# An attention and maxout kernel whose order of work is set by a table per pair of groups

## The chip, the cores and the metric

The kernel runs on one core of one Trainium2 chip. The metric is the device time of one execution in microseconds (us); the median of three runs before the change is 2021.88 us (2021.07 to 2022.24). The core has TensorE (PE, matrix products into PSUM), VectorE (DVE), ScalarE (ACT), GpSimd (POOL, which reaches SBUF only) and SyncE (SP, whose queue issues all DMAs here). Each engine works through its own instructions in program order and waits on semaphores for the others.

## The reference

Pooled attention, and its output goes through a maxout layer:

```python
kv_pool = kv.reshape(B, H // 4, 4, W // 4, 4, C).mean(axis=(2, 4))   # 4 batches, 768 keys of 128
k = v = kv_pool.reshape(B, -1, C) @ w_sr
s = (q @ k.transpose(0, 2, 1)) / sqrt(C)                             # 12288 queries per batch
a = exp(s - s.max(-1)); a /= a.sum(-1) + 1e-09
x = (a @ v).reshape(49152, 128)
h = max(max(x @ w1, x @ w2), x @ w3)                                 # 768 hidden units
out = h @ w_out
```

## The kernel before

**Precision.** PE works on float16 pairs: each float32 operand is split into a high and a low half, and three products (high-high, high-low, low-high) stand for one. The maxout is rewritten with differences against w1, so that two products, a relu and a max give the hidden values, and a product w1 w_out (`w1o`) is added in the projection.

**Tiling.** The queries form 96 groups of 512 (24 per batch); a group has 4 tiles of 128 queries and its hidden layer 6 steps of 128 units. Each piece of work is a short token, and `step` (L851) and `start` (L948) turn a token into instructions:

- S: scores of a tile, 6 matmuls of 384 columns into one of two score buffers (`ps_s`). m: maximum and bias on DVE (`mx`, `nb`). e: exponential on ACT (`a<-ps_s`), which frees the score buffer. c: high half (`ahl<-a`) on ACT, or on DVE where the token has an exclamation mark. l: low half (`ahl<-a,ahl`) on POOL, or on DVE with the mark, and then SP issues the DMA transpose of the tile (`aT<-ahl`).
- X: half of a group's product with the values, 9 matmuls of 512 columns into `ps_x`; it needs the transposes of all four tiles. xh and xl: its high half on ACT and low half on DVE.
- H: a hidden step, 6 matmuls of 512 columns into the two buffers `ps_h`. R: relu of the first on ACT; M: max with the second on DVE; C: high half (`hh`) on ACT; L: low half (`hl`) on POOL, or on DVE with the mark. O: projection of a step, 3 matmuls of 512 columns into `ps_o` (6 at a group's last step).
- P: the finished group is copied out of PSUM by DVE (`o_planes`) and SP issues a DMA transpose of it. G: the two planes are merged by DVE (`o_sb<-o_turned`). T: it is scaled by DVE (`rs`, then `o_sb<-o_sb,w_down,rs`) and stored.
- qd, qc, qp, qe, qh, ql: load of q for two groups, scaling of its columns (POOL), its size (DVE: the largest absolute value), the exponent's scale, and the high and low halves with a DMA transpose (`qT`). k: a part of the preparation of the next batch's keys, by place (`keys_step`, L999). Tokens of `START` that begin with w prepare the weights, and kv, add, fold, gat, end and gathered the first batch's keys.

All instructions of the engines are recorded through one helper, so that nearly all rows of the profile name L103. Matmuls and everything else keep the program's order on each engine (`InOrder`, L95), so the tables set the order.

**Order before.** `START` (L169) brings the first two groups into flight. Then a loop (L1041) goes through groups 2 to 95 and six steps of each; row `g % 2 * 6 + f` of `ORDER` (L155) holds the tokens of that step. Some tokens act on all that is waiting (c, l, C, L), S is left out in steps 1 and 4 and X acts only there, and k looks up what part of the key work belongs to this step: two kv tiles of 512 KB a group, in the first 6 groups of a batch, the sums in its groups 3 to 8.

**The end.** The last group's last hidden step is done in two halves (`last_hidden`, L694). Its projection (`last_project`, L722) has the hidden values as the stationary operand and `w` with both halves as 256 moving columns, so that the sums with w's high half and with its low half stand side by side in PSUM; `last_finish` (L805) copies one out on ACT, adds on DVE, scales and stores. Two projections stand between `last_hidden` and the one that needs its values.

Of the kernel before, what the change touches and what calls it, by code (L numbers as in the profile page):

```python
# [9 lines left out]
F32 = mybir.dt.float32  # L10
# [10 lines left out]
def kernel(  # L21
# [101 lines left out]
    def times(t, src, by, by2=None):  # L123
# [29 lines left out]
    W_SIGNS = 3  # L153
    HB_ = 5
    ORDER = (  # L155
# [12 lines left out]
    )  # L168
    START = (  # L169
# [328 lines left out]
    st = {x: {} for x in ("q", "qr", "ps", "qT", "sc", "sm", "nb", "aT", "x", "hp", "h", "a", "turned", "split", "qhl", "xh")}  # L498
# [13 lines left out]
    def q_peak(s, summed=False):  # L512

        assert s < 2 or next_q["cols"] >= 2 * s + 2
# [207 lines left out]
    def last_project(g, f):  # L722

        (fh, fn), n = divmod(f, NFT // 2), NJ // 2
        h = st["h"].pop((g, f))
        chunks = [(h, wo[fh][:, fn])]
        if f == 0:
            chunks.insert(0, (st["x"][g], w1o))
            st["o"] = [
                ps.rearrange("p (j s c) -> p j s c", s=2, c=C)  # L730
                for ps in (ps_o.tile([C, G], F32, name="ps_o"), ps_x.tile([C, G], F32, name="ps_x"))
            ]
        for part, o in enumerate(st["o"]):
            for m, (h, w) in enumerate(chunks):
                hh, hl = h[part] if isinstance(h, list) else h
                off = 0 if isinstance(h, list) else part * n
                for i, h_ in enumerate((hh, hl)):
                    for j in range(n):
                        mm(
                            out=o[:, j], lhsT=h_[:, (off + j) * P:(off + j + 1) * P], rhs=w,  # L740
                            start=(f == 0 and m == 0 and i == 0 and j == 0),
                            stop=(f == NFT - 1 and i == 1 and j == n - 1),
                        )
# [61 lines left out]
    def last_finish(g, rs):  # L805
        osb, n = op.tile([P, NJ, C], F32, name="o_sb"), NJ // 2
        for part, o in enumerate(st["o"]):
            half = slice(part * n, (part + 1) * n)
            lo = hp.tile([P, G], F32, name="h1", bufs=2)[:, :n * C].rearrange("p (j c) -> p j c", c=C)
            act.copy(out=lo, in_=o[:, :, 1])  # L810
            dve.tensor_tensor(out=osb[:, half], in0=o[:, :, 0], in1=lo, op=ALU.add)
            dve.scalar_tensor_tensor(
                out=osb[:, half], in0=osb[:, half], scalar=w_down,
                in1=rs[:, half].unsqueeze(2).to_broadcast([P, n, C]), op0=ALU.mult, op1=ALU.mult,
            )
            store(g, part * n, osb[:, part * n:(part + 1) * n])
# [17 lines left out]
    to_max, to_exp, to_hi, to_lo, to_merge, to_scale = [], [], [], [], [], []  # L834
    to_relu, to_h, to_hh, to_hl, to_xh, to_xl = [], [], [], [], list(range(NG)), []
    to_hidden, to_project = ([(g, f) for g in range(NG) for f in range(NFT)] for _ in range(2))
    next_q = {"load": 0, "cols": 0, "peak": 0, "exps": 0, "hi": 0, "lo": 0}
    nxt = None

    def turn(what, last):  # L840
        n = next_q[what]
        if n >= last:
            return None
        next_q[what] += 1
        return n

    def some(queue, one):
        for _ in range(1 if one else len(queue)):
            yield queue.pop(0)

    def step(token, g, f, one=False, on=None):  # L851

        if token == "H":
            gf = to_hidden.pop(0)
            hidden(*gf)
            to_relu.append(gf)
        elif token == "R":
            for gf in some(to_relu, one):
                to_h.append((gf, hidden_first()))
        elif token == "M":  # L860
            for gf, h1 in some(to_h, one):
                st["h"][gf] = hidden_max(h1)
                to_hh.append(gf)
        elif token == "C":
            for gf in some(to_hh, one):
                hidden_hi(*gf)
                to_hl.append(gf)
        elif token == "L":
            for gf in some(to_hl, one):
                hidden_lo(*gf, on)  # L870
        elif token == "O":
            project(*to_project.pop(0))
        elif token == "S":
            if (one or f not in (1, 4)) and tiles:
                to_max.append(tiles.pop(0))
                scores(*to_max[-1])
        elif token == "X":
            if (one or f in (1, 4)) and products:
                g, part = products.pop(0)
                (attend if g else attend_tile)(g, part)  # L880
        elif token == "m":
            for t in some(to_max, one):
                soft_max(*t)
                to_exp.append(t)
        elif token == "e":
            for t in some(to_exp, one):
                soft_exp(*t)
                to_hi.append(t)
        elif token == "c":
            for t in some(to_hi, one):  # L890
                soft_hi(*t, on)
                to_lo.append(t)
        elif token == "l":
            for t in some(to_lo, one):
                soft_lo(*t, on)
        elif token == "xh":
            if to_xh:
                attended_hi(to_xh[0])
                to_xl.append(to_xh.pop(0))
        elif token == "xl":  # L900
            for x in some(to_xl, one):
                attended_lo(x)
        elif token == "P":
            if g > 0:
                turn_out(g - 1)
                to_merge.append((g - 1, g * NFT + f))
        elif token in ("G", "T"):
            if token == "G":
                n = g * NFT + f
                while to_merge and (one or to_merge[0][1] < n - 1 or g == NG - 1 and f == NFT - 2):  # L910
                    m = to_merge.pop(0)[0]
                    merge(m)
                    to_scale.append(m)
            else:
                for m in some(to_scale, one):
                    scale_out(m, finish_scale(m))
        elif token == "qd":
            s = turn("load", NG // 2)
            if s is not None:
                q_load(s)  # L920
        elif token == "qc":
            q = turn("cols", NG)
            if q is not None:
                q_cols(q, on)
# [167 lines left out]
```

## Time and profile before

| | |
|---|---|
| median of three runs | 2021.88 us |
| profiled execution, its own time | 2023.5 us |
| its span, first to last instruction | 2021.7 us |
| mean granted TensorE clock | 0.998 |
| busy PE / DVE / ACT / POOL | 98% / 74% / 72% / 70% |
| DMA moved | 283.30 MB, mean 140 GB/s |

The busy share of PE counts each matmul with a modelled end, so it is nearer to 100% than its real occupation. A row of a group of instructions reads: line, engine, operation, output and inputs by the program's names, shapes and count; then the time in which at least one of them ran, the mean of one in ns, and the engine's idle time just before them with what ended it. A row of the timeline starts with its time from the span's start and its length.

### The profile page before, as it was taken

The numbers are of one execution on the slowest core, as the hardware profiler recorded it, in microseconds if no ns is written. First come the engines' busy times: TensorE is split into PE (matmuls) and PEld (weight loads), VectorE is DVE, ScalarE is ACT, GpSimd is POOL, SyncE is SP. The second block draws the span as 40 slices with busy tenths as digits, with TensorE's granted clock in tenths as the row PEclk, the third lists the DMA queues.
The fourth block names the chain that finished last, engine by engine and source line by source line (L and its number), as shares of the span: only waits on it lengthen the run. The fifth ranks groups of instructions, "written<-read, shape, count | busy, mean of one in ns | idle before, by whom it ended". The sixth has DMA issues, their size and how long they took to land.

```text
span 2021.7 us, 29151 instructions
## 1 busy us (share of the span) xinstructions
PE 1971.2 (98%) x9797; PEld 963.3 (48%) x9797; DVE 1503.6 (74%) x2469; ACT 1454.0 (72%) x2530; POOL 1406.7 (70%) x1059
## 2 busy tenths in 40 slices
PE   5899999999999999999999999999999999999998
PEld 4444444444444444444444444444444444444444
DVE  7878877767777886777776888677777777777675
ACT  3767777777777677777777777777777777777774
POOL 2667767777767677777777677767776777777764
PEclk9999999999999999999999999999999999999999
DMA  7697766666677867666767876676666766676662
GB/s 252 124 189 169 140 129 131 137 131 125 139 161 165 171 130 136 129 128 131 141 123 165 169 175 130 120 136 134 138 124 127 136 136 125 126 138 133 130 119 65
DMA packets 839959, 283.30 MB, mean 140 GB/s; under 512 B 813440, under 2 KB 814592, under 8 KB 839808
## 3 DMA queue, kind: packets, MB, share of 16 engines
q1 hardware_dynamic: 839808, 281.43, 68.7%
q8 instruction: 77, 1.26, 0.2%
q14 instruction: 74, 0.61, 0.1%
HBM read 53.54 MB, written 25.17 MB: 39 GB/s over the span
## 4 chain that ended last, share of the span: by engine, by line
PE 80%; DVE 7%; DMA 5%; ACT 4%; issue 2%; POOL 2%; SPq 0%; DVEq 0%; ACTq 0%; POOLq 0%
PE ps_h L103 31%; PE ps_o L103 17%; PE ps_x L103 17%; PE ps_s L103 15%; DMA aT<-ahl 4%; DVE h L103 1%; POOL ahl L103 1%; DVE q_row L103 1%; ACT ahl L103 1%; ACT a L103 1%; DVE mx L103 1%; ACT xh L103 1%; ACT hh L103 1%; ACT h L103 1%; DVE rs L103 1%
## 5 line engine op out<-in xcount | busy, mean ns | idle before, releaser
L103 POOL TENSOR_TENSOR ahl<-a,ahl 128x768 f16<-128x768 f32 x383 | 628.3, 1651 | 305.6 <-issue 170.9
L103 POOL TENSOR_TENSOR hl<-h,hh 128x512 f16<-128x512 f32 x572 | 666.5, 1176 | 179.8 <-ACT hh L103 179.2
L103 DVE SCALAR_TENSOR_TENSOR h<-ps_h,h 128x512 f32<-128x512 f32 x575 | 396.5, 690 | 185.2 <-ACT h L103 94.7
L103 ACT ACTIVATE h<-ps_h 128x512 f32<-128x512 f32 x575 | 341.8, 594 | 247.2 <-PE ps_h L103 243.9
L103 ACT CAST hh<-h 128x512 f16<-128x512 f32 x577 | 349.6, 615 | 165.1 <-DVE h L103 165.0
L103 DVE TENSOR_REDUCE mx<-ps_s 128x1 f32<-128x768 f32 x384 | 366.1, 953 | 112.1 <-PE ps_s L103 111.2
L103 PE MATMUL ps_h<-xh,d_hi 128*128 128x512 f16 x1150 | 436.9, 380 | 2.5 <-DVE w1o L103 2.5
L103 PE MATMUL ps_h<-xh,d_lo 128*128 128x512 f16 x1150 | 436.7, 380 | 0.0
L103 PE MATMUL ps_h<-xl,d_hi 128*128 128x512 f16 x1150 | 436.4, 379 | 0.0
L103 ACT ACTIVATE a<-ps_s,nb,q_sc 128x768 f32<-128x768 f32 x384 | 378.4, 988 | 57.2 <-DVE nb L103 51.9
L103 PE MATMUL ps_x<-aT,v_hi 128*128 128x512 f16 (+1 forms) x1188 | 375.0, 373 | 15.6 <-DMA aT<-ahl 13.8
L103 PE MATMUL ps_s<-k_hi,qT 128*128 128x384 f16 x1536 | 375.3, 326 | 5.7 <-ACT a L103 4.9
L103 PEld LDWEIGHTS <-d_hi 128*128 128x128 f16 x2308 | 226.3, 98 | 257.3 <-issue 2.5
L103 PE MATMUL ps_o<-hh,wo 128*128 128x512 f16 x1140 | 339.0, 379 | 0.0
L103 PEld LDWEIGHTS <-qT 128*128 128x128 f16 x2304 | 225.6, 98 | 196.2 <-issue 8.3
L103 ACT CAST ahl<-a 128x768 f16<-128x768 f32 x379 | 310.3, 832 | 4.8 <-DMA aT<-ahl 0.4
L103 PEld LDWEIGHTS <-wo 128*128 128x128 f16 x1710 | 167.3, 98 | 191.7 <-issue 0.4
L103 PE MATMUL ps_s<-k_lo,qT 128*128 128x384 f16 x768 | 250.8, 327 | 0.3 <-DVE k_lo L103 0.3
L103 PE MATMUL ps_x<-aT,v_lo 128*128 128x512 f16 (+1 forms) x594 | 220.4, 373 | 0.0
L103 PE MATMUL ps_o<-hl,wo 128*128 128x512 f16 x570 | 216.0, 379 | 0.1
L103 POOL TENSOR_TENSOR q_sb<-q_sb,col_row 128x512 f32<-128x512 f32 x94 | 124.3, 1323 | 103.3 <-DMA q_sb<-in_q_dram 103.3
L103 PEld LDWEIGHTS <-v_hi 128*128 128x128 f16 x1188 | 115.4, 98 | 149.6 <-issue 9.6
(136 smaller groups left out, 1413.5 us busy)
## 6 DMA issues: line engine op xcount, KB each, us to landing
q_sb<-in_q_dram SPq DMA_DIRECT2D x48, 512.0 KB, 4.4
kv_piece<-in_kv_dram SPq DMA_DIRECT2D x48, 512.0 KB, 4.8
out_dram<-o_sb SPq DMA_DIRECT2D x95, 256.0 KB, 2.2
aT<-ahl SPq DMA_TRANSPOSE x384, 4.0
kv_piece<-in_moe_w_dram SPq DMA_DIRECT2D x6, 384.0 KB, 6.9
qT<-q_hl SPq DMA_TRANSPOSE x96, 3.4
o_turned<-o_planes SPq DMA_TRANSPOSE x95, 3.3
kv_piece<-in_moe_w_out_dram SPq DMA_DIRECT2D x2, 384.0 KB, 9.3
```

The source lines that it names most:

```text
L103: return lambda **kw: tc.keep_in_program_order(op(**kw))
```

## The change

The loop over groups and `ORDER` go. `START` has another order of the same kinds of work, up to group 4's second score. `STEADY` holds the tokens of one pair of groups and is run 45 times (NG // 2 - 3); `END` holds the rest. Each token now does exactly one piece of work.

The key work is told by two tokens: kd loads one kv tile (groups 1 to 12 of a batch; two kd stand side by side in each pair), and ka does one of three parts a group, by `KEYS_AT`. The sums lie in groups 3 to 15, the rest up to group 19.

The size of q in `STEADY` and `START` is qp!: the sum of absolute values, by an ACT instruction (Abs with accumulation) that the kernel had and did not use. In `STEADY` two of a pair's eight c are on DVE (c!) and two of its twelve L (L!).

In `last_project` the high and low halves of `w` go into the same PSUM region in turn: three products of 128 columns for the two of 256. `last_finish` scales straight from PSUM. Five projections now follow `last_hidden` ahead of the one that needs it.

```diff
-    ORDER = (
-        "H e C l L m k R c M X O S qc",
-        "H C R O G c L m M S l e qc k X",
-        "H l P L C T c R O m M e S X k",
-        "H C L R m M l X S e O c k",
-        "H L S C m l R M O c e X k",
-        "H m C xh l xl R c e M L S O qp k X",
-        "H C m l R M e k c L X O S",
-        "H C G R l L O m M c S k X e",
-        "H l P L k C R T e M m O S X c",
-        "H L C qh R m M l X O S e k ql c",
-        "H L m qh R l M c e X S O k C ql",
-        "H xh m C L xl l c e R M O S X k qd",
-    )
-    START = (
-        "wd.2.1 wm.2.1 sr qd qc! ws.2.1 wl.2.1 qc wd.0.0 qp qd wd.0.1 qh wm.0.1!",
...
+    KEYS_AT = ((3, 5, 6, 7), (8, 9, 10, 11), (12, 13, 14, 15))
+    START = (
+        "sr qd wd.1.1 wm.1.1 qc! ws.1.1 wd.0.1 wm.0.1 wl.1.1 ws.0.1 wd.2.1 wn.1.1 wl.0.1 qc",
+        "qp! wd.2.0 wm.2.1 ws.2.1 wd.3.0 wn.0.1 wr.1.1! wm.3.0 wl.2.1 ws.3.0 wn.2.1 qh wd.1.0 wm.1.0",
+        "ws.1.0 wm.2.0! wr.2.1 wd.0.0 wm.0.0! wl.1.0 ws.2.0 ws.0.0 wl.3.0 wl.0.0 wl.2.0 wn.1.0 kv.0.0 kv.2.0",
+        "kv.2.1 turn_w1.1 wn.0.0 wr.1.0 wt.0.0 wn.2.0 add.2.0.1 wt.1.0 gat.0.0.4 kv.0.1 gat.0.1.4 wr.2.0 kv.2.2 qd",
+        "kv.2.3 qh turn_w1.0 kv.0.3 fold.2.0.2 gat.2.0.2 wt.2.0 dsize.0 wt.2.1 fold.2.2.2! gat.2.2.2 wt.1.1 wt.0.1 dsize.1",
+        "dsized.0 wh.2.0 kv.1.0 kv.0.2 kv.1.1 dsized.1 wh.2.1 wh.1.0 fold.2.3.2.1! gat.2.3.4.0 kv.1.2 kv.1.3 gat.1.0.4 add.0.2.3",
+        "end.0.2.4 wn.3.0 end.2.3.2.1 wd.3.1 ql add.1.1.2 gathered.2 gathered.0 wm.3.1 wo.2.0 ql gathered_peak.0 kd qc",
+        "gat.1.1.4 wo.1.0 ws.3.1 gathered_peak.2 wl.3.1 end.1.3.4 gathered_peak.1 turn_tops qc qp! gathered.1 gathered_project.1 tops sized",
+        "qe qd qh qc gathered_project.0 gathered_hi.0 gathered_project.2 gathered_hi.1 gathered_lo.0 qh gathered_lo.1 S ql S",
...
+    )
+    STEADY = (
+        "H kd kd qc m S ka R c O M L! l H",
+        "G e qp! c S R m M qh l X e C X",
+        "H L O L O O C R c! L m xh xl S",
+        "e c M C H m S R M H e l l C",
+        "m R c e c L O O S ka ka M H L",
+        "P l l m C O R M H ka R M L e",
+        "X H R ql T G C O X T C qh M L!",
+        "L C c! S xh xl H R M O H R m qe",
+        "S l M O C L C ka m L qd ql L H",
+        "R O M e O P c H R l ka e C M",
+        "qc S C",
+    )
+    END = (
...
+        "C H P R M C L L L L L T last_hidden O",
+        "O O G T last_project.3 last_project.4 last_project.5 last_finish",
     )
...
-                ps.rearrange("p (j s c) -> p j s c", s=2, c=C)
-                for ps in (ps_o.tile([C, G], F32, name="ps_o"), ps_x.tile([C, G], F32, name="ps_x"))
+                ps[:, :n * C].rearrange("p (j c) -> p j c", c=C)
+                for ps in (ps_o.tile([P, G], F32, name="ps_o"), ps_x.tile([P, G], F32, name="ps_x"))
...
-                for i, h_ in enumerate((hh, hl)):
+                for i, (h_, s) in enumerate(((hh, 1), (hh, 0), (hl, 0))):
                     for j in range(n):
                         mm(
-                            out=o[:, j], lhsT=h_[:, (off + j) * P:(off + j + 1) * P], rhs=w,
+                            out=o[:, j], lhsT=h_[:, (off + j) * P:(off + j + 1) * P], rhs=w[:, s],
...
-            lo = hp.tile([P, G], F32, name="h1", bufs=2)[:, :n * C].rearrange("p (j c) -> p j c", c=C)
-            act.copy(out=lo, in_=o[:, :, 1])
-            dve.tensor_tensor(out=osb[:, half], in0=o[:, :, 0], in1=lo, op=ALU.add)
             dve.scalar_tensor_tensor(
-                out=osb[:, half], in0=osb[:, half], scalar=w_down,
+                out=osb[:, half], in0=o, scalar=w_down,
...
+    def keys_load(b, r):
+        if r == 1:
+            KT[b] = Keys(b)
+        if r <= KS * R:
+            KT[b].load(*divmod(r - 1, R))
...
+    def keys_step(b, r, n):
+        k = KT.get(b)
+        sums = {
+            KEYS_AT[s][i]: (s, what) for s in range(KS) for i, what in enumerate(((0, 1), (2, 3), (0, 2), "pool"))
+        }
+        if n < KU and r in sums:
+            s, what = sums[r]
+            if what == "pool":
+                k.pool(s, n)
+            else:
+                k.add(s, *what, us=slice(n, n + 1))
+        after = {
+            (KEYS_AT[0][3], 2): lambda: k.peak(0), (KEYS_AT[1][3], 2): lambda: k.peak(1),
+            (12, 2): lambda: k.turn(0), (13, 0): lambda: k.turned(0),
+            (KEYS_AT[2][3], 2): lambda: (k.peak(2), k.turn(1)), (16, 0): lambda: k.turned(1),
+            (16, 2): k and k.turn_tops, (17, 0): k and k.tops, (17, 1): k and k.sized,
+            (17, 2): lambda: k.project(0), (18, 0): lambda: k.projected(0),
+            (18, 2): lambda: k.project(1), (19, 0): lambda: (k.projected(1), k.value(0), k.value(1)),
+        }
...
     KT[0] = Keys(0)
+    run(START)
+    for _ in range(NG // 2 - 3):
+        run(STEADY)
+    run(END)
```

More of the change, by code (lines that the diff above doesn't have):

```diff
@@ L833 @@
     products = [(0, j) for j in range(NJ)] + [(g, part) for g in range(1, NG) for part in range(2)]
[L834 to L856, printed above, removed]
+    steps = [(g, f) for g in range(NG) for f in range(NFT)]
+    halves_q, eights_q = (list(range(n)) for n in (NG, NG // 2))
+    next_keys = [(b, r) for b in range(1, B) for r in range(1, GPB + 1)]
+    todo = {
+        "S": list(tiles), "X": products, "H": steps[:-1], "O": steps[:-3], "P": list(range(NG - 1)),
+        "xh": list(range(NG)), "qd": list(eights_q), "qc": list(halves_q), "qp": list(eights_q),
+        "qe": list(eights_q), "qh": list(halves_q), "ql": list(halves_q), "kd": list(next_keys),
+        "ka": [(b, r, n) for b, r in next_keys for n in range(3)],
+        **{t: [] for t in ("m", "e", "c", "l", "R", "M", "C", "L", "xl", "G", "T")},
+    }
@@ new lines, with step @@
+    FOLLOWS = {"S": "m", "m": "e", "e": "c", "c": "l", "H": "R", "R": "M", "M": "C", "C": "L", "xh": "xl", "P": "G", "G": "T"}
+    def step(token, on=None):
+        if not todo[token]:
+            return
+        n = todo[token].pop(0)
+        if token == "S":
+            scores(*n)
+        elif token == "m":
+            soft_max(*n)
+        elif token == "e":
+            soft_exp(*n)
+        elif token == "c":
+            soft_hi(*n, on)
+        elif token == "l":
+            soft_lo(*n, on)
+        elif token == "X":
+            (attend if n[0] else attend_tile)(*n)
+        elif token == "xh":
+            attended_hi(n)
+        elif token == "xl":
+            attended_lo(n)
+        elif token == "H":
+            hidden(*n)
@@ L857, in step @@
         elif token == "R":
[L858 to L859 removed]
+            st["h1"][n] = hidden_first()
         elif token == "M":
[L861 to L863 removed]
+            st["h"][n] = hidden_max(st["h1"].pop(n))
         elif token == "C":
[L865 to L867 removed]
+            hidden_hi(*n)
@@ L868, in step @@
         elif token == "L":
-            for gf in some(to_hl, one):
-                hidden_lo(*gf, on)
+            hidden_lo(*n, on)
         elif token == "O":
[L872 to L902, printed above, removed]
-        elif token == "P":
[L904 to L916, printed above, removed]
@@ L917, in step @@
+            project(*n)
+        elif token == "P":
+            turn_out(n)
+        elif token == "G":
+            merge(n)
+        elif token == "T":
+            scale_out(n, finish_scale(n))
         elif token == "qd":
-            s = turn("load", NG // 2)
-            if s is not None:
-                q_load(s)
+            q_load(n)
         elif token == "qc":
-            q = turn("cols", NG)
-            if q is not None:
-                q_cols(q, on)
+            q_cols(n, on)
@@ L948, in start @@
     def start(token):
-        nonlocal nxt
         k, on = KT[0], dve if token[-1] == "!" else None
@@ L981, in start @@
             AIDS[name](*n)
-        elif name == "nk":
-            r, f = n
-            if nxt is None:
-                nxt = Keys(1)
-            keys_step(r, f)
         else:
-            step(name, *(n or (1, 0)), one=True, on=on)
+            step(name, on)
     WEIGHTS = {
@@ L1036 @@
-    KT[0] = Keys(0)
-    for row in START:
-        for token in row.split():
-            start(token)
-    for g in range(2, NG):
-        r, b = g % GPB, g // GPB + 1
-        if r == 1 and b < B:
-            nxt = Keys(b)
-        for f in range(NFT):
-            if g == NG - 1 and f == NFT - 1:
-                break
-            for token in ORDER[g % 2 * NFT + f].split():
-                step(token, g, f)
-            if g == NG - 1 and f == NFT - 2:
-                step("G", g, f)
-                step("T", g, f)
-                rs = finish_scale(NG - 1)
-            if nxt and r == 17 and f == 4:
-                KT[b], nxt = nxt, None
@@ L1065, with run @@
+    def run(rows):
+        for row in rows:
+            for token in row.split():
+                start(token)
+    KT[0] = Keys(0)
+    run(START)
+    for _ in range(NG // 2 - 3):
+        run(STEADY)
+    run(END)
+    assert not any(v for t, v in todo.items() if t[0] != "k")
 _INS = ["q", "kv", "w_sr", "moe_w1", "moe_w2", "moe_w3", "moe_w_out"]
```

84 lines of the change are left out of this document (20 added, 64 removed), and 50 rows, old and new, of tables (END, START, STEADY).

## The prediction

> **What bounds the kernel now.** I read the engine totals first, then TensorE's (PE's) busy time in stretches that follow the stages.
>
> ```profile
> PE 1971.2 (98%) x9797; PEld 963.3 (48%) x9797; DVE 1503.6 (74%) x2469; ACT 1454.0 (72%) x2530; POOL 1406.7 (70%) x1059
> ```
> ```profile
> 0.00:39.20 39.20, 21.74 (x139) 20.26 (x140) 30.22 (x64) 8.59 (x17) 8.87 (x12) 1.00 0.82 289
> 39.20:59.00 19.80, 13.53 (x127) 9.45 (x127) 17.08 (x40) 14.32 (x26) 13.06 (x8) 1.00 0.79 143
> 59.00:100.00 41.00, 37.78 (x185) 18.57 (x183) 33.56 (x57) 28.60 (x53) 22.10 (x16) 0.96 0.60 112
> 100.00:590.00 490.00, 485.54 (x2389) 233.88 (x2388) 370.14 (x604) 360.16 (x625) 350.44 (x264) 1.00 0.72 143
> 590.00:700.00 110.00, 105.53 (x510) 50.05 (x509) 86.40 (x134) 76.96 (x135) 78.06 (x58) 0.98 0.82 172
> 700.00:1990.00 1290.00, 1281.51 (x6305) 616.99 (x6304) 949.39 (x1544) 952.01 (x1653) 923.32 (x696) 1.00 0.68 135
> 1990.00:2021.70 31.70, 25.57 (x149) 14.13 (x147) 16.85 (x29) 13.32 (x25) 10.82 (x9) 0.96 0.15 45
> ```
>
> Columns: stretch, length, then busy us of PE, weight loads, VectorE (DVE), ScalarE (ACT), GpSimd (POOL), PE's granted clock, DMA share, GB/s. PE sets the end. Its work hardly changes, so the change can win only PE's idle time: 17.5 us before the first score (39.2), 6.3 to the first hidden step (59), 3.2 to 100, 17.4 in the long middle (4.46 + 4.47 + 8.49), 6.1 at the end: 50.5 in all, plus lost clock (0.96 of 41 us is 1.6 us, 0.98 of 110 is 2.2).
>
> Who ends PE's waits in the middle (first view) and in the first 100 us (second):
>
> ```profile
> PE ps_x L103 <- DMA aT<-ahl: 12.0, 13, 2.5
> PE ps_x L103 <- DVE pool_max L103: 3.4, 3, 1.1
> ```
> ```profile
> PE ps_s L103 <- DVE kv_piece L103: 12.3, 2, 11.0
> PE ps_h L103 <- DVE w1o L103: 2.5, 1, 2.5
> ```
>
> The middle's stalls are X (attend) waiting for the last transpose of the probabilities. The chain of waits shows an unstalled pair of groups, and the late transposes:
>
> ```profile
> 530.79 1.94 PE ps_x L103 x9
> ...
> 570.96 1.94 PE ps_x L103 x9
> 572.91 1.29 PE ps_h L103 x6
> 574.20 0.97 PE ps_s L103 x6
> ...
> 580.04 1.29 PE ps_o L103 x6
> ...
> 638.11 5.55 DMA aT<-ahl
> 679.36 7.16 DMA aT<-ahl
> ```
>
> From the same X of one pair to the next is 40.17 us, and that is all PE work: 12 H of 1.29, 8 S of 0.97, 4 X of 1.94, 10 O of 0.65 and 2 of 1.29. So the repeated table cannot beat 40.17 either. In the queue of SyncE the late transpose stands behind loads:
>
> ```profile
> 675.87 0.89 SPq L103 DMA_DIRECT2D kv_piece<-in_kv_dram  x1
> 676.87 1.25 SPq L103 DMA_TRANSPOSE qT<-q_hl  x1
> 678.17 0.57 SPq L103 DMA_DIRECT2D q_sb<-in_q_dram  x1
> 679.36 2.26 SPq L103 DMA_TRANSPOSE aT<-ahl  x1
> 681.67 1.71 SPq L103 DMA_DIRECT2D kv_piece<-in_kv_dram  x1
> ```
> ```profile
> aT<-ahl SPq DMA_TRANSPOSE x384, 4.0
> ```
>
> The median is 4.0; with a kv tile and q ahead it took 7.16, and the clock fell after it (0.98 in that stretch's row).
>
> **Middle: the repeated table.** Durations that I use:
>
> ```profile
> L103 POOL TENSOR_TENSOR ahl<-a,ahl 128x768 f16<-128x768 f32 x383 | 628.3, 1651 | 305.6 <-issue 170.9
> L103 DVE TENSOR_REDUCE mx<-ps_s 128x1 f32<-128x768 f32 x384 | 366.1, 953 | 112.1 <-PE ps_s L103 111.2
> L103 ACT ACTIVATE a<-ps_s,nb,q_sc 128x768 f32<-128x768 f32 x384 | 378.4, 988 | 57.2 <-DVE nb L103 51.9
> L103 ACT CAST ahl<-a 128x768 f16<-128x768 f32 x379 | 310.3, 832 | 4.8 <-DMA aT<-ahl 0.4
> L103 DVE COPY o_planes<-ps_o 128x1024 uint16<-128x1024 uint16 x95 | 115.9, 1220 | 24.1 <-PE ps_o L103 23.6
> ```
> ```profile
> 2008.81 0.38 PE L103 MATMUL ps_h<-xh,d_hi 128*128 128x512 f16 x1
> ```
> ```profile
> 2009.72 0.60 ACT L103 ACTIVATE h<-ps_h 128x512 f32<-128x512 f32 x1 [1.57 <-PE ps_h L103]
> ```
>
> Even groups: PE work between the group's last S and its first X was 4 H + 2 S + 1 X + O worth 3.9, or 13.0 us; in the new table it is 5 H + 3 S + 2 X + O worth 4.5, or 17.8. The chain m, e, c, l, transpose is 0.95 + 0.2 + 0.99 + 0.2 + 0.83 + 1.65 + 4.0 = 8.8 without queueing, so these waits should vanish.
>
> Odd groups are the tight ones. Their last exponential (row 10 of the table) stands on ACT behind the R of the H before it. From that H's start: R at 0.9 (rows 2008.81 and 2009.72), e at 1.5, c at 2.7, l ends near 5.2. But SyncE takes its issues in program order, and P (turn_out), now in the same row, comes first: its O ends at 3.2, the copy to planes (1.22) near 4.65, its issue about 1.25 (row 676.87), so the last aT is issued at 5.95 and lands at 9.95. X is due after 4 H, 3 S and O worth 2.6: at 10.7. That leaves 0.7 us: a landing of up to 4.7 us is free. No q load stands just ahead any more (it is issued a row earlier, right behind tile 2's transpose), and the two kv tiles of a pair ("kd kd") follow behind. So I expect most of these waits to go as well.
>
> The row 681.67 shows a kv load behind the transpose that took 7.16, which by itself would make kd dangerous; the loads ahead explain it as well. The Trainium skill, page "DMA: Bandwidth & Descriptors", section "Queues, rings and completion order", says that descriptors on one engine are consumed in ring order; by that rule loads behind cost nothing, and without it 18 pairs (36 tiles) would each pay up to 2.5 us.
>
> Two more places have little room. S of tile 3 needs the score buffer of tile 1: ACT does C, R, c and e ahead of it, free at about 3.5, due at 4.2. Each second H half needs M done; the tightest (H 3 of the odd group, behind P and m on DVE) has 0.2. A key sum ("ka") stands ahead of two M's in the same rows. The top reduction of the keys moves behind an S, so the three waits on pool_max (3.4) go.
>
> What the middle can give: 17.4 idle, about 3 that the modelled ends of the waits hide (0.38 a matmul for 0.216 of issue) and some 1.5 of lost clock: 22. Bounds: 0 (each wait stays) and -22. I take **-17**, leaving 5 for the tight places in groups with key work. "VectorE apart from GpSimd" I cost at nothing: it shortens DVE steps such as this one, which no PE wait names.
>
> ```profile
> 1034.93 2.27 POOL L103 TENSOR_TENSOR hl<-h,hh 128x512 f16<-128x512 f32 x2
> ```
> ```profile
> 1036.04 1.19 DVE L103 TENSOR_SCALAR rs<-sm,o_down 128x4 f32<-128x4 f32 x1
> ```
>
> DVE's step over four columns ends just as POOL's two do, at 1037.2. What hides it is PE's 40.17 of work; uncovered, one such 1.19 in each of 46 pairs would cost 55. GpSimd's waits for q, which the earlier issue takes away, are as far from the path: 0.
>
> **qp!** puts the row sums of |q| on ACT (Abs with accumulation over 1024) in place of DVE's 1.21 reduction. No row shows it. Below: DVE gains 1.2, PE nothing. Above: nearest is a<-ps_s, 0.99 + 0.2 for 768; I take 1.2 a pair. Behind it on ACT stand c and R; the next H is 4.9 us of S and X away, so 0. If ACT had to swap function tables, the row is
>
> ```profile
> L103 ACT ACT_TABLE_LOAD x1 | 1.3, 1283 | 0.7 <-PEq L1076 0.7
> ```
>
> twice a pair, 2.6 us, which delays R and the xh that the next group waits for by about 0.5 to 1: 23 to 46 in all. The Trainium skill, page "ScalarE: Activation LUTs", section "Table sets: the hidden batching unit", says that abs is in every set; by it there is no swap, and no run so far shows it.
>
> **Start.** Before the first S, DVE is 30.2 busy. The new table adds there four tops (2.2), sizes (1.6), two d_lo (2.0), one low part, two scales and so on (1.5), and takes away two q reductions (2.4), two folds (1.1), one q scaling (0.7), one top (0.5): net +2.5, 32.7 of the 36.5 that DVE has after its first load at 2.7. One weight load fewer stands ahead of the last kv tile: 0.38 MB at 289 GB/s, 1.4 us. First S near 37.3: -2. After it DVE sheds about 7 of its 17.1 to the first H, where PE idles 6.3: -2.5. The rest to 100 us, with the w1o wait of 2.5: -1.5. **-6**; bounds +7 (the added DVE work in full, and POOL's folds late) and -11.
>
> **End.** Last projection: 56 matmuls of 256 columns become 84 of 128.
>
> ```profile
> 2012.29 0.38 PE L103 MATMUL ps_o<-wo,hh 128*128 128x256 f16 x2
> 2012.51 0.38 PE L103 MATMUL ps_o<-wo,hl 128*128 128x256 f16 x2
> ...
> 2015.89 0.39 PE L103 MATMUL ps_o<-wo,hh 128*128 128x256 f16 x2 [1.37 <-ACT hh L103]
> ...
> 2016.80 0.38 PE L103 MATMUL ps_x<-wo,hl 128*128 128x256 f16 x2
> ```
> ```profile
> 2018.56 0.48 DVE L103 SCALAR_TENSOR_TENSOR o_sb<-o_sb,w_down,rs 128x256 f32<-128x256 f32 x1
> ```
>
> 56 at 0.109 is 6.1; half the columns at half that, 84 x 0.055, is 4.6: -1.5 (0 if weight loads bind). From PE's end (2017.2) to DVE's (2019.04) is 1.85; without copy and add about 0.6: -1.2. The wait of 1.37 came from DVE, which reached the last hidden step late; five projections now stand between that step and the projection that needs it, instead of two: -1.4. Group 94's merge and scaling now stand ahead of the finish on DVE, about 2 us beside those projections. With a third of the lost clock (0.96 of 31.7 is 1.3) I take **-4.5**; bounds -6 and 0.
>
> **Sum.** 2021.7 - 17 - 6 - 4.5 = 1994.2 of span. The profiled execution took 2023.5, 1.8 more than its span and 1.6 more than the median 2021.88, so **1994.4** on the median's scale.
>
> **Rivals.**
> - *B, the stalls stay*: the odd X still waits as often as now. For it: 0.7 us of room. Against: no load ahead. 2021.9 - 6 - 4.5 = 2011.4. Chance 0.13.
> - *C, a slower start*: DVE binds before the first S (+7) with the rest as forecast: 2021.9 + 7 - 17 - 4.5 = 2007.4. For it: 32.7 of 36.5. Chance 0.10.
> - *D, slower*: P's transpose ahead of the last aT makes its landing late in each pair. Each 0.1 above 4.7 costs 46 x 0.1 = 4.6. It decides from 5.3 (28 us); at 5.5 (as row 638.11) 37 us: 2031. For it: the order on SyncE. Against: median 4.0. Chance 0.10, and a further 0.05 for landings near 5.3, which just cancel the gain (2022).
> - *E, ACT swaps tables*: 1994.4 + 35 = 2029. Chance 0.02.
>
> **How the numbers follow.** The forecast has 0.60; its own range is 1987 to 2003. 0.2% is 4 us, about what can be told from no change. Faster: 0.60 + 0.13 + 0.10 = 0.83; same 0.05; slower 0.12. The range reaches over C and B, and below to the middle and the end in full (1994.4 - 5 - 3): 1986 to 2013; what is left out is D, E and the cancelled case (0.17), and a start at its best.
>
> **What would show it.** Right: PE idle in the middle falls from 17.4 to under 6, no ps_x wait on aT above 1 us, pairs of 40.2; first S near 37, first H near 54.5; one table load; the rs steps mostly far below 1.19. Wrong: ps_x waits on aT in each pair (D), ps_s waits on ACT a in the middle (exponentials late), DVE over 95% busy before the first S (C), ACT_TABLE_LOAD some 90 times (E).

## The result and the profile after

The changed kernel took **1989.76 us** (median of 4, 1988.85 to 1990.73) beside 2021.47 for the kernel before on the same chip: ratio **0.9843, 95% interval 0.9826 to 0.986**, so it is faster by about 32 us. The forecast was 1994.4. The profiled execution took 1989.11, with a span of 1987.0.

Engine totals of the profile page, and TensorE's busy time in the forecast's stretches (columns as there; only the last two bounds are moved, so that the last stretch is again the 31.7 us before the end):

```profile
PE 1962.1 (99%) x9825; PEld 961.5 (48%) x9825; DVE 1576.4 (79%) x2611; ACT 1427.3 (72%) x2526; POOL 1313.0 (66%) x965
```
```profile
0.00:39.20 39.20, 23.83 (x158) 20.65 (x159) 33.65 (x83) 14.23 (x27) 12.01 (x15) 1.00 0.89 311
39.20:59.00 19.80, 15.32 (x130) 9.83 (x130) 14.61 (x37) 14.64 (x27) 12.90 (x8) 1.00 0.84 152
59.00:100.00 41.00, 40.81 (x205) 20.03 (x204) 33.47 (x50) 29.19 (x53) 21.80 (x16) 1.00 0.65 111
100.00:590.00 490.00, 489.64 (x2414) 236.35 (x2413) 392.28 (x643) 358.36 (x635) 331.18 (x243) 1.00 0.72 145
590.00:700.00 110.00, 110.00 (x543) 53.07 (x542) 89.57 (x145) 81.10 (x144) 75.36 (x55) 1.00 0.77 160
700.00:1955.30 1255.30, 1254.51 (x6184) 605.80 (x6182) 990.98 (x1619) 916.38 (x1620) 847.57 (x620) 1.00 0.69 138
1955.30:1987.00 31.70, 28.03 (x199) 15.75 (x196) 21.81 (x37) 13.37 (x25) 12.22 (x11) 0.99 0.32 72
```

The idle time of the middle fell from 17.4 us to 1.15 (0.36 + 0 + 0.79), that of the first 100 us from 27.0 to 20.0, that of the end from 6.1 to 3.7, and the lost clock is all but gone.

A modelled end hides part of a wait, and a lower clock makes matmuls longer. So below, "lost" time of a stretch is counted from the matmuls' starts: each gap to the next start beyond what a matmul of its form takes at the full clock in these traces (0.216 us for 512 columns of float16, 0.112 for 128 of float32). By that count the first 100 us lost 33.7 before and 24.8 after, the middle **23.4 before and 2.1 after**, the end 2.3 and 0. The middle gave 21.3 of the 34.7 us by which these two profiled spans differ.

What TensorE still waits for (the four longest groups: total, times, longest), and SyncE's queue in one odd group of the middle:

```profile
PE ps_h L103 <- DVE w_e L103: 5.9, 1, 5.9
PE ps_s L103 <- ACT a L103: 3.2, 3, 1.6
PE ps_h L103 <- DVE sr_e L103: 2.9, 1, 2.9
PE ps_x L103 <- DMA aT<-ahl: 2.8, 4, 1.6
```
```profile
1191.17 1.24 SPq L103 DMA_TRANSPOSE qT<-q_hl  x1
1193.70 1.23 SPq L103 DMA_TRANSPOSE o_turned<-o_planes  x1
1195.02 1.50 SPq L103 DMA_TRANSPOSE aT<-ahl  x1
1196.57 1.58 SPq L103 DMA_DIRECT2D kv_piece<-in_kv_dram  x2
```

Of these waits only two on aT, 1.0 us together and at most 0.7, lie in the middle; the others lie in the first 100 us.

The order in the queue is the one that the forecast read from the table: the finished output's transpose ahead of the tight one, two loads behind. The **room** of an odd group, from the landing of its last aT to the first matmul of X, is 0.9 us in the median (forecast: 0.7 with a landing of 4.0; these land in 3.8). Even groups have 4.7. In the kernel before it was 0.6 (odd) and 0.8 (even).

### The profile page after: what moved, and what is told of

It is laid out like the page before. It is cut to its first block, busy times and chain, and to the rows that moved or that the text cites. A ratio compares the mean times of both kernels' runs of the same rounds, so it can differ in the third digit from the quotient of the medians.

```text
span 1987.0 us, 29527 instructions
## 1 busy us (share of the span) xinstructions
PE 1962.1 (99%) x9825; PEld 961.5 (48%) x9825; DVE 1576.4 (79%) x2611; ACT 1427.3 (72%) x2526; POOL 1313.0 (66%) x965
## 4 chain that ended last, share of the span: by engine, by line
PE 95%; DMA 2%; DVE 1%; POOL 1%; issue 1%; ACT 0%; DVEq 0%; ACTq 0%; POOLq 0%
PE ps_h L103 37%; PE ps_o L103 21%; PE ps_x L103 19%; PE ps_s L103 18%; DMA aT<-ahl 1%; DMA kv_piece<-in_moe_w_out_dram 1%; DVE w_e L103 1%; POOL ahl L103 0%; POOL hl L103 0%; POOL q_sb L103 0%; ACT a L103 0%; ACT hh L103 0%; DMA wsr_sb<-in_w_sr_dram 0%; ACT h L103 0%; DVE o_sb L103 0%
## 5 line engine op out<-in xcount | busy, mean ns | idle before, releaser
L103 POOL TENSOR_TENSOR ahl<-a,ahl 128x768 f16<-128x768 f32 x380 | 639.6, 1683 | 278.7 <-ACT ahl L103 122.4
L103 POOL TENSOR_TENSOR hl<-h,hh 128x512 f16<-128x512 f32 x479 | 559.6, 1177 | 361.5 <-ACT hh L103 361.4
L103 PE MATMUL ps_x<-aT,v_hi 128*128 128x512 f16 (+1 forms) x1188 | 366.7, 373 | 3.0 <-DMA aT<-ahl 2.8
L103 ACT CAST hh<-h 128x512 f16<-128x512 f32 x577 | 339.5, 613 | 30.6 <-DVE h L103 29.7
L103 ACT CAST ahl<-a 128x768 f16<-128x768 f32 x282 | 234.5, 831 | 5.4 <-DMA aT<-ahl 0.9
L103 PEld LDWEIGHTS <-d_lo 128*128 128x128 f16 x1154 | 112.9, 98 | 124.7 <-issue 2.5
```

Of the source, the lines that this page charges most:

```text
L103: return lambda **kw: tc.keep_in_program_order(op(**kw))
```

## The experiments

"Lost" is the middle's lost time as counted above. Times are medians, the kernel before on the same chip beside them.

| run | time | before | ratio, 95% interval | lost |
|---|---|---|---|---|
| e1_loads_ahead | 2068.29 | 2020.24 | 1.0238 (1.0222 to 1.0253) | 78.5 |
| e2_two_tiles | 1991.22 | 2020.24 | 0.9858 (0.9843 to 0.9872) | 4.3 |
| e10_two_turns | 2019.36 | 2020.24 | 0.9999 (0.9989 to 1.0008) | 30.9 |
| e5_engines_back | 1993.08 | 2020.24 | 0.9867 (0.985 to 0.9883) | 6.1 |
| e3_before_one_tile | 2010.47 | 2020.30 | 0.9947 (0.9932 to 0.9962) | 11.7 |
| e3b_before_one_tile_f4 | 2026.04 | 2020.30 | 1.0036 (1.0019 to 1.0052) | 29.2 |
| e4_p_behind | 1987.42 | 2020.30 | 0.9836 (0.9821 to 0.985) | 0.1 |
| e8_after_old_end | 1991.57 | 2020.30 | 0.9856 (0.9839 to 0.9872) | 2.3 |
| e9_before_q_earlier | 2010.78 | 2021.77 | 0.9952 (0.9934 to 0.9969) | 9.5 |
| e13_before_both | 2010.73 | 2021.77 | 0.9952 (0.9934 to 0.997) | 10.6 |
| e11_start_qp | 1991.43 | 2021.77 | 0.9855 (0.9839 to 0.987) | 2.8 |
| e6_qp_on_dve | 1997.32 | 2021.77 | 0.9885 (0.987 to 0.9901) | 11.7 |

### Is it the place of the loads or their spreading?

```diff
 # e1: in STEADY (and kd kd once at START's end)
-"H kd kd qc m S ka R c O M L! l H",   "R O M e O P c H R l ka e C M",
+"H qc m S ka R c O M L! l H",         "R O M e O P c H R kd kd l ka e C M",
 # e2: keys_load
-if r <= KS * R: KT[b].load(*divmod(r - 1, R))
+for m in (2 * r - 2, 2 * r - 1):
+    if m < KS * R: KT[b].load(*divmod(m, R))
```

> The changed kernel with one move: the two kv loads of a pair of groups (kd kd) stand just ahead of the odd group's last transpose of the probabilities in SyncE's order, not behind it. Number and size of the loads stay. Theory (place in the queue decides): in the 18 pairs that load keys, that transpose is issued about 1.6 us later and lands later still, as in the kernel before, where it took 5.3 to 7.2 us with a kv tile and q ahead; with 0.9 us of room that is 1.5 to 3.5 us a pair, +27 to +63 us on 1989.8, so 2017 to 2053, and the waits of ps_x on aT stand in just those pairs. Rival (one tile per group, the spreading, brought the gain, wherever the load stands): within 4 us of 1989.8.

> The changed kernel with two kv tiles per group again, in the first six groups of a batch and not one in each of twelve; the loads keep their place behind the tight transpose, so a loading pair has four of them in a row there. Theory (place decides): the next transpose behind them has 4 us and more of room, so 0 to +3 us on 1989.8. Rival (spreading brought the gain): the middle's waits come back, +10 to +16 us, 2000 to 2006.

The place. In e1 the loads stand ahead of the tight transpose in 19 pairs (two loads in 14 of them, one in 5). Moving them these few tokens forward cost 80 us (1.0238 against 0.9843), more than the whole change gained and more than I had expected at most. Two tiles per group in the right place (e2) cost 3 by ratio, with overlapping intervals, at the upper edge of what place alone allowed and far from 10 to 16. In e1 the waits and one loading pair (queue, first matmuls of X, windows with busy time and granted clock) read:

```profile
PE ps_x L103 <- DMA aT<-ahl: 35.3, 16, 3.6
PE ps_x L103 <- issue: 15.9, 5, 3.9
```
```profile
697.20 1.23 SPq L103 DMA_TRANSPOSE o_turned<-o_planes  x1
698.48 1.24 SPq L103 DMA_DIRECT2D kv_piece<-in_kv_dram  x2
699.82 7.17 SPq L103 DMA_TRANSPOSE aT<-ahl  x3
```
```profile
706.09 0.59 PE L103 MATMUL ps_x<-aT,v_hi 128*128 128x512 f16 x1 [2.72 <-DMA aT<-ahl]
706.47 0.63 PE L103 MATMUL ps_x<-aT,v_lo 128*128 128x512 f16 x1
706.90 1.06 PE L103 MATMUL ps_x<-aT,v_hi 128*128 128x512 f16 x2
```
```profile
706.10:709.20 3.10, 3.10 (x8) 1.08 (x8) 1.64 (x3) 0.90 (x2) 2.64 (x3) 0.53 0.96 192
709.20:711.40 2.20, 2.20 (x12) 0.97 (x11) 0.00 (x0) 0.00 (x0) 1.30 (x1) 1.00 0.00 0
```

The waits in the loading pairs come to 49.2 us (the other 2.0 of these rows lie before 100 us). The other part of the 80 is in the last lines: after a wait of 2.7 the matmuls start 0.43 apart, at a granted clock of 0.53, for 3.1 us. TensorE was busy 1991.4 us in e1 and 1962.1 in the changed kernel with the same 9825 matmuls: 29 us more, nearly all of it lower clock (the mean granted clock is 0.986 beside 1.000), which my expectation had left out.

By the ring-order rule that the forecast took from the Trainium skill, page "DMA: Bandwidth & Descriptors", section "Queues, rings and completion order", loads behind cost nothing. The trace agrees: in the middle of the changed kernel the last aT of an odd group lands 3.8 us after its issue in the median, with two loads behind it (14 groups) and with none (26).

The same question from the other side, in the old table:

```diff
-if f in (1, 4) and 1 <= r <= 6:  m = 2 * (r - 1) + f // 4; n.load(m // R, m % R)
+if f == 1 and 1 <= r <= 12:      n.load((r - 1) // R, (r - 1) % R)     # e3; f == 4 in e3b
 # both: sums at r 5 6 9 10 13 14, peak 15, turns 11 and 15, tops and projections 16 to 19, values 20
```

> The kernel before, with its old table, in which a group loads one kv tile in each of the first twelve groups of a batch and no longer two in each of the first six. The load stands in the second row of a group, behind the last transpose of the probabilities that the odd X waits for; the sums, turns and projections of the keys come two to six groups later. Theory (place decides): the ten stalls that had a kv tile ahead lose it (12.2 us together in the trace of before, of which the q load alone, 0.7 each in four other groups, keeps some 6 in the eight odd ones), so -4 to -10 us with lost clock on 2021, 2011 to 2017. Rival (spreading decides): the same gain, so this run alone doesn't tell them apart; the next one does.

> As the run before it, but the one load of a group stands in the fifth row of each, ahead of the last transposes of the probabilities. Theory (place decides): now eighteen odd groups and eighteen even ones, in place of nine and nine, have a kv tile ahead; ten such stalls cost 12.2 us, so about +8 to +16 us on 2021 with lost clock: 2025 to 2037, slower than before. Rival (spreading decides): as fast as the run with the load behind, within 3 us of it.

By ratio the same spreading is 10.7 us faster behind the transposes and 7.3 slower ahead of them. The waits over the whole run, e3 first, then e3b (in the middle 4.9 and 12.9 us of those on aT, beside 12.0 before):

```profile
PE ps_x L103 <- DMA aT<-ahl: 6.6, 9, 1.7
```
```profile
PE ps_x L103 <- DMA aT<-ahl: 15.4, 20, 2.0
PE ps_x L103 <- issue: 4.1, 4, 1.7
```

e3's gain is just beyond the favourable end of its expectation, e3b's rise just under the least that I had expected. Spreading as such explains no more than the 3 us of e2.

### What of the middle's gain is the queue's order?

e3 waits at the odd X almost only where q's load stands just ahead. So q's load alone was moved (e9), and both together (e13).

```diff
-"H l P L k C R T e M m O S X c",      "H xh m C L xl l c e R M O S X k qd",
+"H l P L k C R T e M m O S X c qd",   "H xh m C L xl l c e R M O S X k",
```

> The kernel before with one move: the load of the next q (qd) stands three rows earlier in the odd half of its table, so it no longer stands just ahead of the odd group's last transpose of the probabilities; the kv tiles stay where they are. Theory (whatever stands just ahead in SyncE's queue decides, q loads as much as kv tiles): the four stalls that had q and no kv tile ahead (2.9 us in the trace of before) go, and the eight that had both (11.0) lose about half, so -4 to -11 us on 2020.3: 2009 to 2016. Rival (the kv tiles alone make the transposes late): within 3 us of 2020.3.

> The kernel before with both: one kv tile per group, behind the last transpose of the probabilities (as in the run that gave 2010.5 beside 2020.3), and the load of q three rows earlier. The old table is otherwise kept. Theory (the order in SyncE's queue is nearly all of the middle's gain): the odd groups' stalls left in that run, 7.0 us, all with q ahead, go too, with some lost clock: 2003, between 2000 and 2007, and the waits of ps_x on aT are under 2 us together. Rival (the new table's longer distances are needed): 2008 or more, waits of ps_x on aT of 4 us or more.

e9 came out as expected, at the favourable end: moving one token brought 10 us by ratio in the old table. It took more from the eight stops with both loads ahead than the half that I had expected: by starts they had lost 11.0 us, and in e9 they lose 1.4, though a kv tile still stands two places ahead. e13 missed: its waits on aT were nearly gone, as the theory had it, but its time is that of the rival and no better than e9's:

```profile
PE ps_s L103 <- DMA qT<-q_hl: 3.9, 6, 1.7
PE ps_x L103 <- DVE pool_max L103: 3.4, 3, 1.1
PE ps_x L103 <- DMA aT<-ahl: 1.0, 2, 0.6
```

The scores now wait for q's own transposes (3.9 us, against 1.0 in e9); the waits on pool_max are those of before. So in the old table these moves in the queue alone take the middle's lost time from 23.4 to 9.5 or 10.6, which is 60 to 65% of what the change took (to 2.1). No order that was tried in the old table brought the rest; in the new table neither the waits on q's transposes nor those on pool_max are left.

### Is the tight place real, and what makes it tight?

```diff
 # e10, turn_out, after the first transpose: the same planes once more, into a tile that nobody reads
+again = op.tile([P, 2, NJ, C], U16, name="o_again", bufs=1)
+sp_dma.dma_start_transpose(
+    out=again.rearrange("p w j c -> p (w j) c"), in_=planes.rearrange("c w t -> c (w t)")
+)
 # e4, STEADY
-"R O M e O P c H R l ka e C M",
+"R O M e O c H R l P ka e C M",
```

> The changed kernel, in which each group's output is transposed twice, the second time into a tile that nobody reads. It puts one more transpose, some 1.3 us of issue, ahead of the odd group's last transpose of the probabilities. Theory (that transpose is the tight one, with 0.9 us of room in the median): the rooms read from the changed kernel's trace, less 1.25 us, give stalls of 22 us over 47 odd groups; less 1.0 us 12, less 2.0 us (if the transposes also hinder one another) 54. So 2012, between 2002 and 2044, with waits of ps_x on aT in most odd groups and none in even ones (4.7 us of room). Rival (no tight place is left, and the forecast's 0.7 us is a number without a meaning): within 4 us of 1989.8.

> The changed kernel, in which the transpose of the finished output (P) stands behind the odd group's last transpose of the probabilities in SyncE's order, not ahead of it, in the repeated table; VectorE's order and all else stay. Theory (P ahead is what makes that place tight): the median room of the odd groups goes from 0.9 us to about 2.2, the three stalls there (1.4 us by starts) go, so -1.4 us on 1989.8, between -2.5 and +0.5; no ps_x wait on aT is left in the middle. Rival (the last exponential or the low part sets that landing, P does not): room and time unchanged.

e10 lost 28.8 more than the changed kernel and is 31 us slower (0.9999 against 0.9843), above the middle of its expectation and inside the range: the whole gain is gone with one more transpose in the queue of each group. 43 of 48 odd groups had no room left, no even one lacked it:

```profile
PE ps_x L103 <- DMA aT<-ahl: 19.6, 31, 1.7
PE ps_x L103 <- issue: 5.8, 12, 1.2
```

So the room of 0.9 is what it seemed, and rival D of the forecast (late each pair) was 1.3 us away. In e4 the median room rose to 1.9 and the least to 0.4; what it lost in the middle fell from 2.1 to 0.1 us, and the span from 1987.0 to 1985.2. That is the best time of all the runs, but its interval overlaps that of the changed kernel: the trace shows the odd X's four stops gone (1.8 us; the expectation had counted three), the times don't prove a faster kernel.

### The parts that I costed at nothing

```diff
 # e5, STEADY
-"H kd kd qc m S ka R c O M L! l H", "H L O L O O C R c! L m xh xl S",
+"H kd kd qc m S ka R c O M L l H",  "H L O L O O C R c L m xh xl S",
-"X H R ql T G C O X T C qh M L!",   "L C c! S xh xl H R M O H R m qe",
+"X H R ql T G C O X T C qh M L",    "L C c S xh xl H R M O H R m qe",
 # e6, STEADY: the |q| sums on VectorE again
-"G e qp! c S R m M qh l X e C X",
+"G e qp c S R m M qh l X e C X",
```

> The changed kernel, in which the repeated table's two low parts of the hidden steps and its one high part of the probabilities that were put on VectorE go back to the engines that do the others: GpSimd for the low parts (+2.4 us of its 40.2 us a pair), ScalarE for the high part (+0.8). This undoes part of what sets VectorE's steps on SBUF apart from GpSimd's. Theory (the engines behind PE have cover; forecast 0 for this part): within 4 us of 1989.8, the waits in the middle unchanged. Rival (setting the two engines apart brings the middle's gain): at least +10 us, with waits of PE on hl, hh, a or aT in each pair.

> The changed kernel, in which the repeated table's row sums of |q| are VectorE's reduction again (45 times) and not ScalarE's. Theory (forecast: 0 on the path for either engine, since PE's work covers both): within 1.5 us of the changed kernel, 40.2 us a pair as before. Rival (the 1.2 us of VectorE stand ahead of a step that PE waits for): 0.5 to 1.2 us in each of 45 pairs, +22 to +54 us.

One of the two is not nothing, and for the other the trace suggests it. e6 is 8.5 us slower by ratio (0.9885 against 0.9843) and lost 9.6 more in the middle; outside both ranges that I had named, too much for 0 and too little for a stop in each pair. The place, on VectorE and TensorE in one of these pairs:

```profile
226.78 1.25 DVE L103 TENSOR_TENSOR kv_piece<-kv_piece 128x512 f32<-128x512 f32 x1
227.96 0.68 DVE L103 SCALAR_TENSOR_TENSOR h<-ps_h,h 128x512 f32<-128x512 f32 x1
228.56 1.57 DVE L103 TENSOR_TENSOR hl<-h,hh 128x512 f16<-128x512 f32 x1
230.04 2.18 DVE L103 COPY o_sb<-o_turned 128x1024 uint16<-128x1024 uint16 x1
232.12 1.20 DVE L103 TENSOR_REDUCE q_row<-q_sb 128x1 f32<-128x1024 f32 x1
...
233.81 0.94 DVE L103 TENSOR_REDUCE mx<-ps_s 128x1 f32<-128x768 f32 x1
234.78 0.21 DVE L103 TENSOR_SCALAR nb<-mx,q_sc 128x1 f32<-128x1 f32 x1
234.91 0.68 DVE L103 SCALAR_TENSOR_TENSOR h<-ps_h,h 128x512 f32<-128x512 f32 x1
```
```profile
235.65 0.38 PE L103 MATMUL ps_h<-xh,d_hi 128*128 128x512 f16 x1 [0.30 <-DVE h L103]
```

VectorE works through from a key sum to the h that the second half of an H needs, and comes 0.47 us late by starts. By starts the middle has 17 such stops for h, 7.3 us together, 13 of them 0.47 and four about 0.3; the changed kernel has none above 0.12. Of the 45 pairs, 15 have a key sum ahead of the reduction, and 14 of these stop; in the fifteenth the merge took 0.73 and not 2.18. Of the 30 pairs without a key sum three stop, and there a step of the keys' projection (`k_lo`, 0.60) stands ahead. So the reduction with a low part and the merge ahead of it is covered; with a key sum as well it is not.

e5 is just past its expectation: 4.9 us slower by ratio, 4.0 more lost, the intervals overlap. Its edit gives back two high parts a pair, not the one that the expectation names. In 22 of its pairs TensorE stops 0.14 us at one H for h of VectorE, and once 0.43, which the changed kernel's don't. One of them, first VectorE, then ScalarE:

```profile
130.31 1.75 DVE L103 SCALAR_TENSOR_TENSOR o_sb<-o_sb,w_down,rs 128x512 f32<-128x512 f32 x1
...
134.58 0.69 DVE L103 SCALAR_TENSOR_TENSOR xl<-ps_x,xh 128x512 f16<-128x512 f32 x1 [1.91 <-ACT xh L103]
```
```profile
133.22 0.83 ACT L103 CAST ahl<-a 128x768 f16<-128x768 f32 x1
133.95 0.59 ACT L103 ACTIVATE xh<-ps_x 128x512 f16<-128x512 f32 x1
```

The scaling took 1.75, with GpSimd's low parts beside it, where the changed kernel has 0.75; so the h and the hh behind it come later, the high part that is back on ScalarE stands ahead of xh, VectorE waits for xh, and its next h is late. All 23 have this wait of 1.91. That speaks for a small price, 0.2% of the time and a tenth of the change, which the times by themselves don't prove; the low parts and the high parts were not tried apart.

### The end and the start

```diff
 # e8: last_project and last_finish as in the kernel before, the new order kept
-for i, (h_, s) in enumerate(((hh, 1), (hh, 0), (hl, 0))):    # rhs=w[:, s]
+for i, h_ in enumerate((hh, hl)):                            # rhs=w
...
+act.copy(out=lo, in_=o[:, :, 1])
+dve.tensor_tensor(out=osb[:, half], in0=o[:, :, 0], in1=lo, op=ALU.add)
 # e11, START: in three rows
-qp!
+qp
```

> The changed kernel with the old last projection and finish: 56 matmuls of 256 columns into regions that keep high and low parts apart, then a copy on ScalarE and an addition on VectorE for each half. The order of the table's end stays new. Theory (forecast's terms): +1.5 for the matmuls and +1.2 for copy and addition, 0 for the wait that the new order already covers: +2.7, between +1.8 and +3.5, so 1992.5 on the scale of 1989.8. Rival (VectorE's other work, the merge and scaling of the group before, ends last there anyway): +0 to +1.5.

> The changed kernel, in which the row sums of |q| of the start (three of them, two ahead of the first score) are VectorE's reduction again and not ScalarE's accumulation. It adds 1.2 us to VectorE twice before the first score. Theory (VectorE sets the first score, as it is busy 33.65 of the first 39.2 us): the first score comes at 37.3 to 38.5 and not at 36.0, and the time rises by 1.0 to 2.5 us. Rival (TensorE's gathers of the kv tiles or the loads set it): first score within 0.4 us of 36.1, time within 0.7 us of that of the changed kernel.

e8: from the first matmul of the last hidden step to the end of the span are 12.1 us (from 1977.62) against 9.8 (from 1977.16): **+2.3**, inside the range. Counted from there, TensorE's last matmul starts 1.4 later and VectorE's last step 2.6. The finish of the changed kernel, then of e8:

```profile
1982.50 0.75 DVE L103 SCALAR_TENSOR_TENSOR o_sb<-o_sb,w_down,rs 128x512 f32<-128x512 f32 x1
1983.17 0.48 DVE L103 SCALAR_TENSOR_TENSOR o_sb<-ps_o,w_down,rs 128x256 f32<-128x256 f32 x1
1983.57 0.48 DVE L103 SCALAR_TENSOR_TENSOR o_sb<-ps_x,w_down,rs 128x256 f32<-128x256 f32 x1
```
```profile
1985.27 0.42 DVE L103 TENSOR_TENSOR o_sb<-ps_o,h 128x256 f32<-128x256 f32 x1 [1.05 <-ACT h L103]
...
1986.58 0.48 DVE L103 SCALAR_TENSOR_TENSOR o_sb<-o_sb,w_down,rs 128x256 f32<-128x256 f32 x1
```

In the changed kernel VectorE comes to the finish straight from the scaling of group 94, in e8 it waits 1.05 for ScalarE's copy: the rival (its other work ends last) holds in the changed kernel alone, so there the finish gained 2.3 where 2.7 had been counted.

e11: the first score starts at 38.24 and not at 35.98, the span is 2.7 longer, the ratio 0.0012 (2.4 us) higher. So VectorE sets the first score, and what it sheds there reaches the end nearly undiminished: of the 2.7, 2.0 are lost in the first 100 us and 0.7 in the middle. This is shown for these two reductions only.

## Why the prediction was right, and where not

The time lay 4.6 us under the forecast, and the forecast's three terms carry it: by the count from the starts and the end's own stretch, the middle, the start and the end gave 21.3, 8.8 and 4.6 us, which make up the 34.7 of the spans. By its steps:

- **The bound.** Right: 27 of the middle's pairs take 40.17 to 40.2 us, none less, and TensorE is 99% busy.
- **Middle, -17.** Right in mechanism, too small: -21.3 by starts. Of the 22 that I had counted as available I left 5 for tight places; they cost 2.1. Late aT in four odd groups, 1.8 of it, is what remained at the odd X. These four transposes landed 4.8 to 5.5 us after their issue, and no other odd one of the middle landed later than the 4.7 that I had called free. Why the four were late stays open: no load stood just ahead of them. The mechanism is shown from both sides (e1, e10, e3 with e3b, e9). I had called only the transpose tight and had not seen that in the old table the q load alone was worth 10 us.
- **Loads behind cost nothing.** Right (e1, and 3.8 us with them and without). The loads behind lie in 20 pairs, five of them with one tile, not in 18 pairs with two.
- **Rivals.** B, C and E didn't come: four stops at the odd X in place of 13, the first score at 36.0, one table load. D, the order on SyncE, didn't come either, but not by much: e10 is that rival, at 2019.4 us, and e4 shows the room that moving P would add.
- **VectorE set apart from GpSimd: 0.** The step that failed is "which no PE wait names": no wait of the old table named these steps, but the new table puts them ahead of one, by the trace of e5 for 0.14 us in 22 pairs. rs did fall far below 1.19 (mean 0.286, from 0.707), but other steps of VectorE beside GpSimd grew, the merge from 0.77 to 1.17 and the key sums from 0.79 to 1.27, and VectorE's total, with the steps moved to it, rose from 1503.6 to 1576.4 (1449.6 in e5, which gives them back). Both rows are of the changed kernel, by groups (busy, mean ns of one):

```profile
L103 DVE COPY o_sb<-o_turned 128x1024 uint16<-128x1024 uint16 x95 | 111.3, 1172 | 0.0
L103 DVE TENSOR_SCALAR rs<-sm,o_down 128x4 f32<-128x4 f32 x96 | 27.4, 286 | 0.0
```

- **qp! on ScalarE: 0.** Wrong by some 8 us, as e6 shows. "DVE gains 1.2, PE nothing" looked for cover on ScalarE, where the step went, and not on VectorE, where it would have stayed; the forecast had named a key sum ahead of two M's and didn't add the two. Its length was right, and there is no table swap:

```profile
L103 ACT ACTIVATE q_abs<-q_sb 128x1024 f16<-128x1024 f32 x48 | 51.0, 1063 | 0.2 <-POOL q_sb L103 0.2
L103 ACT ACT_TABLE_LOAD x1 | 1.3, 1283 | 0.7 <-PEq L1022 0.7
```

The first row and 0.21 for reading the sum make 1.27, for 1.2 taken. That abs needs no table of its own (the Trainium skill, page "ScalarE: Activation LUTs", section "Table sets: the hidden batching unit") agrees with the single load in this trace.

- **Start, -6.** Right in sign and inside its bounds, a third too small, and its parts not right: the first score came at 35.98 (37.3 forecast), the first hidden step at 55.86 (54.5 forecast, 59.05 before), and the first 100 us lost 8.8 less. My -2 was a shorter load queue ahead of the last kv tile; e11 shows that VectorE binds there. Which of the reordered steps brought the first score 3.3 us forward wasn't tried.
- **End, -4.5.** Right. From the first hidden step of the last group after its X to the end of the span it was 24.76 (1996.94 to 2021.7) and is 22.14 (1964.86 to 1987.0), with three projections of 0.65 more in it: -4.6. The 84 matmuls run 0.056 apart, as taken; the wait of 1.37 is gone.

## What to carry to other kernels

Where one queue carries urgent transposes and bulk loads, list for each urgent item what is issued just ahead of it: moving a load by a few tokens was worth between 10 and 80 us here, while spreading the same loads was worth at most 3. When a step is moved off an engine, ask what that engine would be late with if it stayed, adding all that stands ahead in the same row, and not only whether the new engine has cover. A median room smaller than one issue in the same queue (0.9 against 1.3 us) is good only as long as nothing is added.

## What was unexpected of the hardware

- **A stop of TensorE has a price after it.** Of the stops of at least 0.7 us in the middle of before, e1 and e3b, none of the 35 up to 2.1 us was followed by slower matmuls beyond 0.2 us; of the 16 of 2.6 us or more (up to 4.0), 15 were followed by about 3 us at half the clock and cost a further 1.4 to 2.9 us. In e1 this is a third of the loss.
- **VectorE's copy of the turned output** (two-byte parts, in SBUF alone) takes 0.73 to 2.20 us for the same shape, and GpSimd works beside the long ones; the copy of planes out of PSUM is steady at 1.22. Engines and minimum, median and maximum in ns, changed kernel:

```profile
L103 DVE COPY o_sb<-o_turned x95: 733/742/2197, 106.6 to 1981.4; 128x1024 uint16<-128x1024 uint16 x95
```

That GpSimd is the cause of the longer ones was read from overlaps and not isolated by a run.
